# The norm's per-token scalars on VectorE: one-column operations with pointer scalars in place of four-column operations on two tensors

## The chip, the cores and the metric

The kernel runs on one core of one Trainium2 chip. The metric is the device time of one execution in microseconds (us). A core has TensorE (PE, matrix products into PSUM), VectorE (DVE), ScalarE (ACT), GpSimd (POOL), SyncE (SP, which here only issues DMAs) and DMA queues; each engine works through its own instructions in order and waits for semaphores of the others.

## What is computed

Three stages follow one another on 8 batches of 3072 tokens with 256 features: a filter in the frequency domain along the sequence, a feed-forward block whose activation is a softmax times its input followed by a layer norm without bias, and a feed-forward block that takes the maximum of three products.

```
X = np.fft.rfft(x, axis=1);  Y = X * F;  x = np.fft.irfft(Y)     # x: 8 x 3072 x 256
h = x @ w_in                                                      # 24576 x 1024
e = np.exp(h - max(h));  sm = e / (sum(e) + 1e-9)
solu = h * sm
ln = (solu - mean(solu)) / np.sqrt(var(solu) + 1e-6) * g_ln
x = ln @ w_out                                                    # 24576 x 256
h = max(x @ w1, x @ w2, x @ w3)                                   # 24576 x 768
out = h @ w_out2                                                  # 24576 x 256
```

The change touches the second stage: the small per-token numbers that stand in for the softmax's sum and the norm's variance.

## The kernel before, in words

**Tiling.** The sequence transform is done as products with small tables (items a, b, c, d). Six groups of 512 tokens make a batch, so there are 48 groups, numbered t = 0 to 47. For each group there are four h items of 128 tokens each (h0 to h3; `h_item`, L444), two z items (the product with the first w_out, L540), six m items (the three products with w1, w2, w3, L557) and two o items (the output, L587). Values are carried as two fp16 halves, so one logical product is three matmuls.

**What one h item does.** Twelve matmuls fill a PSUM tile `hps` (L461 to L463; one such buffer). VectorE takes its row maximum (L472) and scales it (L475); ScalarE forms the exponential and its row sum into `st[:, 0]` (L478). VectorE makes the scale of the product, `st[:, 1]` and `mx[:, 0]`, from the maximum with four one-column operations (L482 to L485) and multiplies: `u` (L489). Then the statistics of `u` (L493, L494), and the variance is copied into column i of `st[:, 2]` (L495). After h3 the four columns of the group are combined in three operations on 128 x 4 elements (L497 to L499), whose operands lie in SBUF: L497 reads `st[:, 0]` and `st[:, 1]`, L498 reads `st[:, 3]` twice, L499 reads `st[:, 4]` and `st[:, 2]`. GpSimd raises `st[:, 5]` to the power -0.5 (L500), multiplies by a constant (L585), and the o items use the result as a scale when ScalarE evicts them (L601).

**The other users of the same engines.** ScalarE makes the high half `uh` of `u` (L508) and GpSimd the low half `ul` (L509, two tensors of 128 x 1024 in SBUF). Of an m item, ScalarE evicts the first product into `am` (L574), VectorE takes the maximum with the other two (L576, twice), ScalarE makes the high half of `h` (L579) and GpSimd the low half (L580, two tensors in SBUF; for the last m item VectorE does it).

**The d item.** It fills two PSUM tiles `dps` (L424 to L426), which ScalarE (L432) and VectorE (L433, the low half of `y`) read. They come out of a ring of six PSUM tiles that the m, z, o and transform items share. So a later m item finds its PSUM tile free only when L433 has read the d item's tile: PE's matmuls of line L568 then wait for `y` L433.

**The order.** The order in which items are issued for a group is a string of the kernel, `z0 s0 z1 s1 h2 m0 x0 x0 x1 m1 x0 x0 m2 s2 x2 h3 m3 d m4 m5 g0 f o0 s3 o2 g1 s4`, in which s are steps of the next batch's transform, and g0, g1 are the items h0 and h1 of the group after next. In the code the statistics of an h item (`bn`, L491) are held until the next h item. The order on each engine is not that of the code: a scheduler places each operation by its priority and by when its inputs are expected, when the program is built. A change in a few operations can therefore move others.

Of the kernel before, what the change touches and what calls it, by code (L numbers as in the profile page):

```python
# [13 lines left out]
ALU = mybir.AluOpType  # L14
# [16 lines left out]
def kernel(  # L31
# [19 lines left out]
    V, S, G, PE, SP = nc.vector, nc.scalar, nc.gpsimd, nc.tensor, nc.sync  # L51
# [37 lines left out]
    def rtile(name):  # L89
        return ps_r.tile([128, 512], F32, tag="r", name=name)  # L90
# [353 lines left out]
    def h_item(b, g, i):  # L444
        y = y_t[b, g]
        sc = scl[b]
        if i == 0:
            st_t[b, g] = tiny.tile([128, 8, 4], F32, tag="st", name="st", bufs=3)
        st = st_t[b, g]
        if (b, g, i) in ((0, 0, 1), (0, 0, 3)):  # L450

            parts = [rtile("hps0"), rtile("hps1")]
        else:
            parts = [ps_h.tile([128, 1024], F32, tag="h", name="hps")]
        n = len(parts)
        tk = slice(i * 128, (i + 1) * 128)
        for f in range(2):
            o = parts[f % n][:, f * 512 * (2 - n):f * 512 * (2 - n) + 512]
            w = slice(f * 512, (f + 1) * 512)
            for dc in range(2):  # L460
                PE.matmul(o, y[:, dc, 0, tk], win[:, 0, dc, w], start=(dc == 0), stop=False)  # L461
                PE.matmul(o, y[:, dc, 0, tk], win[:, 1, dc, w], start=False, stop=False)  # L462
                PE.matmul(o, y[:, dc, 1, tk], win[:, 0, dc, w], start=False, stop=(dc == 1))  # L463
        u = two.tile([128, 1024], F32, tag="u", name="u")
        mx = tiny.tile([128, 4], F32, tag="mx", name="mx")
        mv = tiny.tile([128, 14], F32, tag="mv", name="mv")
        c1 = slice(i, i + 1)
        us = [u[:, k * 1024 // n:(k + 1) * 1024 // n] for k in range(n)]

        def early():  # L470
            for k, ps in enumerate(parts):
                V.tensor_reduce(mx[:, k:k + 1], ps, axis=AX.X, op=ALU.max)  # L472
            if n > 1:
                V.tensor_tensor(mx[:, 0:1], mx[:, 0:1], mx[:, 1:2], op=ALU.max)
            V.tensor_scalar(mx[:, 1:2], mx[:, 0:1], sc[:, 2:3], None, op0=ALU.mult)  # L475
            sums = [st[:, 0, c1], mx[:, 2:3]]
            for k, ps in enumerate(parts):
                S.activation(us[k], ps, AF.Exp, bias=mx[:, 1:2], scale=sc[:, 1:2], accum_out=sums[k])  # L478
            if bn_held[0]:
                bn_held[0]()  # L480
            bn_held[0] = bn
            V.tensor_scalar(st[:, 1, c1], mx[:, 0:1], sc[:, 1:2], 1.0, op0=ALU.mult, op1=ALU.max)  # L482
            V.tensor_tensor(st[:, 1, c1], st[:, 1, c1], mx[:, 1:2], op=ALU.max)
            V.reciprocal(st[:, 1, c1], st[:, 1, c1])
            V.tensor_scalar(mx[:, 0:1], st[:, 1, c1], sc[:, 3:4], None, op0=ALU.mult)  # L485
            if n > 1:
                V.tensor_tensor(sums[0], sums[0], sums[1], op=ALU.add)
            for k, ps in enumerate(parts):
                V.scalar_tensor_tensor(us[k], ps, mx[:, 0:1], us[k], op0=ALU.mult, op1=ALU.mult)  # L489

        def bn():  # L491
            for f in range(2):
                V.bn_stats(mv[:, 6 * f:6 * f + 6], u[:, f * 512:(f + 1) * 512])  # L493
            V.bn_aggr(mv[:, 12:14], mv[:, 0:12])  # L494
            V.tensor_copy(st[:, 2, c1], mv[:, 13:14])  # L495
            if i == 3:
                V.scalar_tensor_tensor(st[:, 3], st[:, 0], 1e-9, st[:, 1], op0=ALU.add, op1=ALU.mult)  # L497
                V.tensor_tensor(st[:, 4], st[:, 3], st[:, 3], op=ALU.mult)  # L498
                V.scalar_tensor_tensor(st[:, 5], st[:, 4], 1e-6 * 2.0 ** 26, st[:, 2], op0=ALU.mult, op1=ALU.add)  # L499
                G.tensor_tensor(st[:, 6], st[:, 5], mhalf, op=ALU.pow)  # L500

        def late():
            if i == 0:
                ln_t[b, g] = two.tile([128, 2, 8, 512], F16, tag="ln", name="ln")
            ln = ln_t[b, g]
            uh = two.tile([128, 1024], F16, tag="uh", name="uh")
            ul = two.tile([128, 1024], F16, tag="ul", name="ul")
            S.activation(uh, u, AF.Copy)  # L508
            (V if (b, g, i) == (0, 0, 3) else G).tensor_tensor(ul, u, uh, op=ALU.subtract)  # L509
            SP.dma_start_transpose(out=ln[:, 0, :, tk], in_=uh)  # L510
            SP.dma_start_transpose(out=ln[:, 1, :, tk], in_=ul)
        return early, late

    def z_parts(b, g):
# [520 lines left out]
    def h(i):  # L1035
        run(h_item(0, 0, i))
        flush()
# [67 lines left out]
    for t in range(NT):  # L1105
# [8 lines left out]
        def h(i):  # L1114
            if nxt:
                run(h_item(*nxt, i))
# [9 lines left out]
        for w in (ORDER if t else FIRST).split():  # L1126
            k, i = w[0], int(w[1:] or 0)
            if k == "h":
                h(i)
            elif k == "g" and nx2:  # L1130
                run(h_item(*nx2, i))
            elif k == "z":
                run(z_item(b, c, i))
                if i == 0:
                    fill(3)
            elif k == "m":
                m(i)
            elif k == "s":
                fft(i)
            elif k == "o":  # L1140
                run(o_item(b, c, i))
            elif k == "d" and nx2:
                run(d_item(*nx2))
            elif k == "f":
                flush()
            elif k == "x":
                if i == 0:
                    fill(1)
                    if not jobs and NB > 1 and 1 not in x_t and t == 0:
                        for k in range(6):  # L1150
                            load_x(1, k)
                if i == 1 and nx2 and nx2[1] == 0:
                    flush()
                    load_d(*nx2)
                if i == 2:
                    fin(b, c)
# [125 lines left out]
```

## Time and profile before

| | |
|---|---|
| time, median of 3 runs (lowest to highest) | 2904.94 us (2900.44 to 2908.57) |
| the profiled execution | 2904.83 us, of which its span from the first to the last instruction 2903.1 us |
| PE busy | 2804.4 us (97%) |
| DVE busy | 2048.4 us (71%) |
| ACT busy | 1236.9 us (43%) |
| POOL busy | 1139.9 us (39%) |
| granted TensorE clock, mean of the span | 0.992 of the upper level, 2.4 GHz |

PE is busy nearly all the time, so the views that matter are those that say where PE stands idle and who ends that idle time. A row of the waits names the engine, the operation that waited and what it waited for; a row of the timeline gives an operation's start, its duration, and in brackets the idle time of its engine ahead of it. In the timeline consecutive operations of one engine overlap a little, since they are pipelined.

### The profile page before, as it was taken

The numbers are of one execution on the slowest core, as the hardware profiler recorded it, in microseconds if no ns is written. First come the engines' busy times: TensorE is split into PE (matmuls) and PEld (weight loads), VectorE is DVE, ScalarE is ACT, GpSimd is POOL, SyncE is SP. The second block draws the span as 40 slices with busy tenths as digits, with TensorE's granted clock in tenths as the row PEclk, the third lists the DMA queues.
The fourth block names the chain that finished last, engine by engine and source line by source line (L and its number), as shares of the span: only waits on it lengthen the run. The fifth ranks groups of instructions, "written<-read, shape, count | busy, mean of one in ns | idle before, by whom it ended". The sixth has DMA issues, their size and how long they took to land.

```text
span 2903.1 us, 49134 instructions
## 1 busy us (share of the span) xinstructions
PE 2804.4 (97%) x18923; PEld 1561.0 (54%) x18924; DVE 2048.4 (71%) x3918; ACT 1236.9 (43%) x2024; POOL 1139.9 (39%) x1208
## 2 busy tenths in 40 slices
PE   8789899999999999999999999999999999999999
PEld 7544455555555555555555555555555555555555
DVE  7877668677777777777677767867777667656663
ACT  5644444344443344444444444434444344434332
POOL 5433553344334442344334433344432434323322
PEclk9999999999999999999999999999999999999999
DMA  8446885587467764677555875567844566422321
GB/s 256 107 102 166 146 177 156 102 138 130 104 157 125 134 116 106 162 126 130 113 146 121 134 125 118 153 110 134 136 110 107 112 137 117 92 66 52 62 48 29
DMA packets 718378, 352.71 MB, mean 121 GB/s; under 512 B 620544, under 2 KB 663936, under 8 KB 718144
## 3 DMA queue, kind: packets, MB, share of 16 engines
q1 hardware_dynamic: 689040, 242.57, 43.7%
q0 software_dynamic: 28960, 106.95, 15.0%
q8 instruction: 148, 2.42, 0.3%
q14 instruction: 86, 0.70, 0.1%
q10 hardware_dynamic: 144, 0.07, 0.0%
HBM read 126.13 MB, written 71.30 MB: 68 GB/s over the span
## 4 chain that ended last, share of the span: by engine, by line
PE 76%; DVE 11%; issue 4%; DMA 4%; POOL 3%; ACT 2%; SPq 0%; POOLq 0%; ACTq 0%; DVEq 0%
PE mps L568 10%; PE mps L570 9%; PE mps L569 9%; PE zps L548 5%; PE zps L551 5%; PE zps L549 5%; PE hps L461 5%; PE hps L462 5%; PE hps L463 5%; PE ops L596 4%; PE ops L597 4%; PE ops L595 4%; DVE st L497 2%; DVE am L576 2%; DVE mx L472 1%
## 5 line engine op out<-in xcount | busy, mean ns | idle before, releaser
L509 POOL TENSOR_TENSOR ul<-u,uh 128x1024 f16<-128x1024 f32 x191 | 408.2, 2137 | 1049.3 <-ACT uh L508 901.2
L568 PE MATMUL mps<-z,wm 128*128 128x512 f16 x1728 | 657.1, 380 | 45.2 <-DVE y L433 36.9
L569 PE MATMUL mps<-z,wm 128*128 128x512 f16 x1728 | 657.3, 380 | 0.0
L570 PE MATMUL mps<-z,wm 128*128 128x512 f16 x1728 | 657.1, 380 | 0.0
L576 DVE SCALAR_TENSOR_TENSOR am<-mps,am 128x512 f32<-128x512 f32 x576 | 393.7, 684 | 191.3 <-PE mps L570 96.3
L472 DVE TENSOR_REDUCE mx<-hps 128x1 f32<-128x1024 f32 (+1 forms) x194 | 234.5, 1209 | 213.3 <-PE hps L463 213.2
L579 ACT ACTIVATE h<-am 128x512 f16<-128x512 f32 x288 | 180.5, 627 | 464.1 <-DVE am L576 464.0
L580 POOL TENSOR_TENSOR h<-am,h 128x512 f16<-128x512 f32 x240 | 278.4, 1161 | 206.4 <-ACT h L579 205.8
L478 ACT ACTIVATE u<-hps,mx,scl 128x1024 f32<-128x1024 f32 (+1 forms) x194 | 231.7, 1195 | 290.5 <-DVE mx L475 242.1
L597 PE MATMUL ops<-wo,h 128*128 128x256 f16 x1152 | 314.1, 273 | 0.8 <-POOL h L580 0.8
L595 PE MATMUL ops<-wo,h 128*128 128x256 f16 x1152 | 314.0, 273 | 0.7 <-ACT o L601 0.6
L596 PE MATMUL ops<-wo,h 128*128 128x256 f16 x1152 | 314.1, 273 | 0.0
L461 PE MATMUL hps<-win,y 128*128 128x512 f16 x768 | 294.1, 383 | 13.3 <-ACT y L436 7.4
L569 PEld LDWEIGHTS <-wm 128*128 128x128 f16 x1728 | 169.4, 98 | 250.9 <-issue 58.2
L489 DVE SCALAR_TENSOR_TENSOR u<-hps,mx,u 128x1024 f32<-128x1024 f32 (+1 forms) x194 | 246.5, 1271 | 74.1 <-ACT u L478 72.9
L462 PE MATMUL hps<-win,y 128*128 128x512 f16 x768 | 294.0, 383 | 0.0
L463 PE MATMUL hps<-win,y 128*128 128x512 f16 x768 | 293.2, 382 | 0.0
L548 PE MATMUL zps<-ln,wo 128*128 128x512 f16 x752 | 285.8, 380 | 0.4 <-ACT o L601 0.4
L549 PE MATMUL zps<-ln,wo 128*128 128x512 f16 x752 | 285.7, 380 | 0.0
L508 ACT ACTIVATE uh<-u 128x1024 f16<-128x1024 f32 x192 | 202.8, 1056 | 192.8 <-DVE u L489 191.8
L570 PEld LDWEIGHTS <-wm 128*128 128x128 f16 x1728 | 169.5, 98 | 205.4 <-issue 2.7
L568 PEld LDWEIGHTS <-wm 128*128 128x128 f16 x1728 | 169.4, 98 | 199.8 <-issue 2.4
(233 smaller groups left out, 4500.3 us busy)
## 6 DMA issues: line engine op xcount, KB each, us to landing
out_dram<-o SPq DMA_DIRECT2D x95, 256.0 KB, 2.3
ft<-in_filt_dram POOLq DMA_DIRECT2D x56, 384.0 KB, 7.0
xt<-in_x_dram POOLq DMA_DIRECT2D x42, 512.0 KB, 8.4
scr_a<-ao SPq DMA_DIRECT2D x42, 512.0 KB, 3.3
bin<-scr_a POOLq DMA_DIRECT2D x56, 384.0 KB, 6.1
scr_z<-zt SPq DMA_DIRECT2D x56, 384.0 KB, 3.0
din<-scr_z POOLq DMA_DIRECT2D x42, 512.0 KB, 5.1
bt<-in_dft_b_dram POOLq DMA_DIRECT2D x56, 144.0 KB, 3.3
```

The source lines that it names most:

```text
L461: PE.matmul(o, y[:, dc, 0, tk], win[:, 0, dc, w], start=(dc == 0), stop=False)
L462: PE.matmul(o, y[:, dc, 0, tk], win[:, 1, dc, w], start=False, stop=False)
L463: PE.matmul(o, y[:, dc, 1, tk], win[:, 0, dc, w], start=False, stop=(dc == 1))
L548: PE.matmul(ps, wo1[:, 0, c, w], ln[:, 0, c], start=(c == 0), stop=False)
L549: PE.matmul(ps, wo1[:, 1, c, w], ln[:, 0, c], start=False, stop=False)
L568: PE.matmul(pss[k], wm[k][:, 0, dc, w], z[:, dc, 0], start=(dc == 0), stop=False)
L569: PE.matmul(pss[k], wm[k][:, 1, dc, w], z[:, dc, 0], start=False, stop=False)
L570: PE.matmul(pss[k], wm[k][:, 0, dc, w], z[:, dc, 1], start=False, stop=(dc == 1))
L576: V.scalar_tensor_tensor(am, ps, 2.0 ** -15, am, op0=ALU.mult, op1=ALU.max)
L595: PE.matmul(o, h2[:, j, 0, tk], wo2[:, 0, j], start=(j == 0), stop=False)
L596: PE.matmul(o, h2[:, j, 0, tk], wo2[:, 1, j], start=False, stop=False)
L597: PE.matmul(o, h2[:, j, 1, tk], wo2[:, 0, j], start=False, stop=(j == 5))
```

## The change

```
-            V.tensor_scalar(st[:, 1, c1], mx[:, 0:1], sc[:, 1:2], 1.0, op0=ALU.mult, op1=ALU.max)
-            V.tensor_tensor(st[:, 1, c1], st[:, 1, c1], mx[:, 1:2], op=ALU.max)
+            V.tensor_scalar(st[:, 1, c1], mx[:, 0:1], sc[:, 1:2], mx[:, 1:2], op0=ALU.mult, op1=ALU.max)
+            V.tensor_scalar(st[:, 1, c1], st[:, 1, c1], 1.0, None, op0=ALU.max)
             V.reciprocal(st[:, 1, c1], st[:, 1, c1])
...
             for k, ps in enumerate(parts):
                 V.scalar_tensor_tensor(us[k], ps, mx[:, 0:1], us[k], op0=ALU.mult, op1=ALU.mult)
+            V.tensor_scalar(st[:, 3, c1], st[:, 0, c1], 1e-9, st[:, 1, c1], op0=ALU.add, op1=ALU.mult)
+            V.tensor_scalar(st[:, 4, c1], st[:, 3, c1], st[:, 3, c1], 1e-6 * 2.0 ** 26, op0=ALU.mult, op1=ALU.mult)
 
         def bn():
...
             V.bn_aggr(mv[:, 12:14], mv[:, 0:12])
-            V.tensor_copy(st[:, 2, c1], mv[:, 13:14])
+            V.tensor_scalar(st[:, 5, c1], mv[:, 13:14], st[:, 4, c1], None, op0=ALU.add)
             if i == 3:
-                V.scalar_tensor_tensor(st[:, 3], st[:, 0], 1e-9, st[:, 1], op0=ALU.add, op1=ALU.mult)
-                V.tensor_tensor(st[:, 4], st[:, 3], st[:, 3], op=ALU.mult)
-                V.scalar_tensor_tensor(st[:, 5], st[:, 4], 1e-6 * 2.0 ** 26, st[:, 2], op0=ALU.mult, op1=ALU.add)
                 G.tensor_tensor(st[:, 6], st[:, 5], mhalf, op=ALU.pow)
```

The three four-column operations of a group become three one-column operations of each h item: the second input is given as a pointer scalar (one value for each partition), so each reads one tensor. The same is done to L483: the maximum with `mx[:, 1]` moves into L482 as its second pointer scalar. The new lines are L490, L491 (behind `u`) and L497 (behind the aggregate, in place of the copy); line numbers from L495 on shift: statistics are L495 and L496 in the new kernel, the maximum of an m item is L575, the low half of its last item L579.

The order on VectorE ahead of `y` L433, in a group of the steady part, before (st: the small numbers, mv: statistics, am: an m item's maximum):

```order
L576 SCALAR_TENSOR_TENSOR am<-mps,am 128x512
L493 BN_STATS mv<-u 128x6 x2
L497 SCALAR_TENSOR_TENSOR st<-st 128x4
L494 BN_AGGR mv<-mv 128x2
L498 TENSOR_TENSOR st<-st 128x4
L495 COPY st<-mv 128x1
L433 TENSOR_TENSOR y<-dps,y 128x512 x2
L499 SCALAR_TENSOR_TENSOR st<-st 128x4
```

and the same place in the changed kernel, behind `u` L489:

```order
L490 TENSOR_SCALAR st<-st 128x1
L575 SCALAR_TENSOR_TENSOR am<-mps,am 128x512
L491 TENSOR_SCALAR st<-st 128x1
L495 BN_STATS mv<-u 128x6 x2
L433 TENSOR_TENSOR y<-dps,y 128x512 x2
L496 BN_AGGR mv<-mv 128x2
L497 TENSOR_SCALAR st<-mv,st 128x1
```

Ahead of `y` the two operations on four columns, the aggregate and the copy are gone, and two one-column operations have come.

The order on VectorE in the first group (t = 0) around `u` of h3, before (xm: maxima of the next batch's input, which wait for its load):

```order
L484 RECIPROCAL st<-st 128x1
L111 TENSOR_REDUCE xm<-xt 128x1
L485 TENSOR_SCALAR mx<-st,scl 128x1
L497 SCALAR_TENSOR_TENSOR st<-st 128x4
L111 TENSOR_REDUCE xm<-xt 128x1
L489 SCALAR_TENSOR_TENSOR u<-hps,mx,u 128x1024
```

and the same place in the changed kernel, from `u` on:

```order
L489 SCALAR_TENSOR_TENSOR u<-hps,mx,u 128x1024
L490 TENSOR_SCALAR st<-st 128x1
L575 SCALAR_TENSOR_TENSOR am<-mps,am 128x512
L491 TENSOR_SCALAR st<-st 128x1
L495 BN_STATS mv<-u 128x6 x2
L111 TENSOR_REDUCE xm<-xt 128x1
```

The reductions of the next batch's input stood ahead of `u` and now stand behind it. On PE the order of items is the same from group 1 on; in the first group and ahead of it some matmuls trade places with their neighbours.

## Rows read from the trace of the kernel before

**Rows 1.** The page: span, and busy time, share, instructions of each engine.

```profile
span 2903.1 us, 49134 instructions
PE 2804.4 (97%) x18923; PEld 1561.0 (54%) x18924; DVE 2048.4 (71%) x3918; ACT 1236.9 (43%) x2024; POOL 1139.9 (39%) x1208
```

**Rows 2.** Waits of PE, whole span: us in total, times, longest us.

```profile
PE mps L568 <- DVE y L433: 36.9, 26, 2.9
PE hps L461 <- ACT y L436: 7.4, 1, 7.4
PE bps L242 <- DMA bin<-scr_a: 6.8, 1, 6.8
PE hps L461 <- DVE u L489: 6.0, 3, 4.2
```

**Rows 3.** Timeline of PE at three of these waits: start, duration, [idle before].

```profile
560.87 0.38 PE L568 MATMUL mps<-z,wm 128*128 128x512 f16 x1 [1.54 <-DVE y L433]
...
1023.18 0.38 PE L570 MATMUL mps<-z,wm 128*128 128x512 f16 x1
1025.08 0.38 PE L568 MATMUL mps<-z,wm 128*128 128x512 f16 x1 [1.52 <-DVE y L433]
...
2356.40 0.58 PE L568 MATMUL mps<-z,wm 128*128 128x512 f16 x1 [2.93 <-DVE y L433]
```

**Rows 4.** Timeline of DVE ahead of the first of them.

```profile
1017.08 0.21 DVE L475 TENSOR_SCALAR mx<-mx,scl 128x1 f32<-128x1 f32 x1
1017.21 0.20 DVE L482 TENSOR_SCALAR st<-mx,scl 128x1 f32<-128x1 f32 x1
1017.44 0.16 DVE L483 TENSOR_TENSOR st<-st,mx 128x1 f32<-128x1 f32 x1
...
1020.45 1.28 DVE L493 BATCH_NORM_STATS2 mv<-u 128x6 f32<-128x512 f32 x2
1021.64 1.61 DVE L497 SCALAR_TENSOR_TENSOR st<-st 128x4 f32<-128x4 f32 x1
1023.18 0.20 DVE L494 BATCH_NORM_AGGREGATE mv<-mv 128x2 f32<-128x12 f32 x1
1023.30 1.07 DVE L498 TENSOR_TENSOR st<-st 128x4 f32<-128x4 f32 x1
1024.29 0.14 DVE L495 COPY st<-mv 128x1 f32<-128x1 f32 x1
1024.36 1.27 DVE L433 TENSOR_TENSOR y<-dps,y 128x512 f16<-128x512 f32 x2
```

**Rows 5.** Timeline of POOL at the same time.

```profile
1021.12 2.12 POOL L509 TENSOR_TENSOR ul<-u,uh 128x1024 f16<-128x1024 f32 x1 [4.73 <-ACT uh L508]
1023.20 1.15 POOL L580 TENSOR_TENSOR h<-am,h 128x512 f16<-128x512 f32 x1
```

**Rows 6.** Timeline of ACT: the high half of y, there and in another group.

```profile
1021.45 1.06 ACT L432 ACTIVATE y<-dps 128x512 f16<-128x512 f32 x2
...
500.17 1.06 ACT L432 ACTIVATE y<-dps 128x512 f16<-128x512 f32 x2
```

**Rows 7.** Timeline of DVE in that other group, where POOL did not compute.

```profile
500.36 0.15 DVE L497 SCALAR_TENSOR_TENSOR st<-st 128x4 f32<-128x4 f32 x1
500.61 0.11 DVE L498 TENSOR_TENSOR st<-st 128x4 f32<-128x4 f32 x1
500.79 1.28 DVE L433 TENSOR_TENSOR y<-dps,y 128x512 f16<-128x512 f32 x2
```

**Rows 8.** The small operations: count, ns min/median/max, first and last start, forms.

```profile
L482 DVE TENSOR_SCALAR st<-mx,scl x192: 160/204/207, 96.5 to 2839.7; 128x1 f32<-128x1 f32 x192
L485 DVE TENSOR_SCALAR mx<-st,scl x192: 198/214/216, 98.0 to 2840.3; 128x1 f32<-128x1 f32 x192
L495 DVE COPY st<-mv x192: 140/153/156, 101.2 to 2847.3; 128x1 f32<-128x1 f32 x192
L497 DVE SCALAR_TENSOR_TENSOR st<-st x48: 145/1616/3453, 126.2 to 2844.6; 128x4 f32<-128x4 f32 x48
L498 DVE TENSOR_TENSOR st<-st x48: 107/1068/1076, 126.4 to 2846.3; 128x4 f32<-128x4 f32 x48
```

**Rows 9.** The first group: timeline of PE, then of DVE.

```profile
179.72 0.61 PE L461 MATMUL hps<-win,y 128*128 128x512 f16 x1 [4.20 <-DVE u L489]
```

```profile
175.71 1.22 DVE L111 TENSOR_REDUCE xm<-xt 128x1 f32<-128x1024 f32 x1 [1.20 <-DMA xt<-in_x_dram]
178.38 1.27 DVE L489 SCALAR_TENSOR_TENSOR u<-hps,mx,u 128x1024 f32<-128x1024 f32 x1
```

## Prediction

> **What bounds the kernel now.** The first view is the table of busy times: PE works 2804.4 of 2903.1 us, VectorE 2048.4 [rows 1]. VectorE as a whole is not the bound, so what the change takes from or gives to its busy time counts for nothing by itself; only operations that stand ahead of something PE waits for count. PE is idle for 2903.1 - 2804.4 = 98.7 us, and that is the most that any change off PE can win. The second view, the waits of PE, says who ends that idle time: 36.9 us in 26 waits for `y` L433, and otherwise single waits of the start and of the first batch, 7.4, 6.8 and 6.0 us [rows 2]. The third view is the timeline around one of the 26. PE ran out of work behind a matmul begun at 1023.18 and went on at 1025.08, idle for 1.52 us; the longest such wait is 2.93 us, and of the others none is over 1.54 us [rows 3]. What VectorE did meanwhile: the statistics at 1020.45, then L497, which took 1.61 us for four elements per partition, the aggregate, L498 with 1.07 us, the copy, and at 1024.36 `y` [rows 4]. PE waits for work of which two tiny operations are the largest part.
>
> Why do they take so long? GpSimd's `ul` runs from 1021.12 to 1023.24, and L497 ends at 1021.64 + 1.61 = 1023.25; GpSimd's L580 runs from 1023.20 to 1024.35, and L498 ends at 1023.30 + 1.07 = 1024.37 [rows 4, 5]. Both operations end with a GpSimd operation on two SBUF tensors. In a group where GpSimd did not compute at that moment, L497 took 0.15 us and L498 0.11 us [rows 7]. So an operation of VectorE with two SBUF tensors is held until GpSimd's is through. The one-tensor operations show nothing of it: in 192 cases each, L482 never took more than 0.207 us, L485 0.216 us, the copy L495 0.156 us, where L497 has a median of 1.616 us [rows 8].
>
> **The change part by part.** *What leaves the path to `y`.* From the end of the statistics (L497 starts at 1021.64) to `y` (1024.36) VectorE spent 2.72 us [rows 4]. In the new order all four operations of that stretch are gone from it: L497 and L498 don't exist any more, the aggregate and what follows it stand behind `y`.
>
> *What is added to it.* L490 and L491 stand ahead of `y`. Each has one tensor and one pointer scalar, like L482, and takes a place of 0.13 us (from L475 at 1017.08 to L482 at 1017.21) [rows 4]: 0.26 us for both. L482 now reads `mx[:, 1]`, which L475 has written just before; a step that depends on the one ahead takes 0.23 us (L482 at 1017.21, L483 at 1017.44) instead of 0.13 [rows 4], so 0.10 us more. Its second pointer scalar has no row of its own: from below it is free, and from above I take the whole duration of such an operation again, 0.2 us [rows 8]; I take nothing, since L482 with one pointer and a constant is no longer than L485 with one pointer alone. L483 with a constant in place of a tensor stays at one place. So VectorE is ready for `y` at 1021.64 + 0.26 + 0.10 = 1022.00.
>
> *What is late next.* `y` needs ScalarE's high half. ScalarE begins that at 1021.45 [rows 6]; where VectorE was early, `y` began 500.79 - 500.17 = 0.62 us behind it [rows 6, 7]. ScalarE itself follows `u`, which L482 makes 0.10 us later. So `y` begins at 1021.45 + 0.10 + 0.62 = 1022.17, not 1024.36: 2.19 us sooner. 25 of the 26 waits are at most 1.54 us and go entirely, with 0.65 us to spare; of the one of 2.93 us 0.74 us is left. Gain: 36.9 - 0.74 = 36.2 us. The spare 0.65 us also covers the 0.2 us that a second pointer might cost. In the groups without a wait nothing is won.
>
> *The other h items.* Each gets 0.13 us twice behind `u` and 0.10 us ahead of it. PE waits for `u` only 6.0 us in 3 waits, all in the first group and ahead of it [rows 2], so in the steady part the time before the next h item hides them. If that cover were gone, 0.36 us x 192 = 69 us would be at stake, but the row of PE's waits names no such wait. The last combination is now one column behind the aggregate instead of L499, off PE's path.
>
> *The first group.* The scheduler also moves other work there. Before, `u` of h3 stood behind reductions of the next batch's input that waited for a load (1.20 us at 175.71), `u` came at 178.38, and PE stood 4.20 us until 179.72 [rows 9]. In the new order the reductions stand behind `u`. The most that this wins is 4.2 us; but PE then comes sooner to the next batch's first item, which waited 6.8 us for its load already [rows 2], so the time may be given back. From below I allow a loss of one more wait of that kind, 6.8 us. I take half of the gain, 2.1 us.
>
> *The sum.* The profiled execution took 2904.83 us, 1.7 us more than its span and within 0.2 us of the median 2904.94, so it stands for it. 2904.8 - 36.2 - 2.1 = 2866.5 us.
>
> **One rule against the change.** The rows show no one-tensor operation held by GpSimd [rows 8]. The Trainium skill, page "SBUF — State Buffer", section "Who interferes with whom", agrees on operations with two SBUF inputs, but says that copies and `tensor_scalar` too can enter a mode that uses both ports and then contend with GpSimd. By that rule the new operations would be held as well, and the sum would be rival C's; by the rows it is the forecast. 192 copies and 384 `tensor_scalar` of one column speak against it here.
>
> **The rivals.** *B, half of it.* ScalarE becomes the bound of `y`: its high half of `y` is already the last to be ready, 0.17 us behind VectorE, and its queue is in order. If PE, now without pauses, finds it about 1.4 us later than in the old phase, then 0.75 us of a typical wait of 1.42 (36.9 / 26) comes back: 26 x 0.75 = 19 us, and the time is about 2886. Against it: ScalarE is busy 43% [rows 1] and is fed by PE, so it moves along with it.
>
> *C, the stall stays.* The one-column operations are held by GpSimd like the old ones, and L490 and L491 pay ahead of `y` what L497 and L498 paid (1.54 and 0.99 us as places in the timeline). Then `y` begins 2.72 - 2.53 - 0.10 = 0.09 us sooner, the gain is 26 x 0.09 = 2.3 us, and the time 2904.8 - 2.3 - 2.1 = 2900.4, no measurable change. The change would then not do what it says. For it: nothing but the rule above. Against it: [rows 8], and that GpSimd begins `ul` only at 1021.12, behind the place of the new pair.
>
> *D, slower.* A pointer scalar that an operation just ahead has written could cost more than a tensor read: VectorE might have to fetch it only when the write has landed. The place is L482, L490 and L491 of each h item; no row shows such a pair alone. Ahead of `y` three such reads stand, so with a price p each the 2.19 us are used up at p = 0.73 us, and at p = 1.0 us `y` is 0.81 us later than before: 26 x 0.81 = 21 us, 2904.8 + 21 - 2 = 2924. It decides from p = 0.85 on, at which the loss leaves the noise. Against it: L485, which reads what the reciprocal has just written, as a tensor, takes 0.214 us in all [rows 8].
>
> *E, more.* The first group keeps all of its 4.2 us and some of its other waits shrink: 2860 or less.
>
> **How the numbers follow.** About 0.3% (8.7 us) is what a measurement of this kernel can tell from no change. The forecast, 2861 to 2873, has 73%; E, below it, 6%; B, 2874 to 2896, 12%; C 5%; D 4%. Faster by over 0.3% (below 2896) is the forecast with B and E, 91%; within it C, 5%; slower D, 4%. The range 2857 to 2879 holds the forecast's cases, nearly all of E and the nearer part of B, some 80%; its lower end is 36.9 + 4.2 us plus the 6.8 us of the first batch's load, its upper end the forecast with a loss of 6.8 us in the start and a few tenths of a us left at each wait.
>
> **What would show it.** In the profile after: PE's waits for `y` fall from 36.9 us to a few us; the timeline shows statistics, then `y`, some 2.2 us sooner against PE; no small operation on `st` over 0.3 us beside GpSimd's `ul`; L490 and L491 at about 0.2 us each in 192 cases. The sum is wrong if the 26 waits stay with another name (B: ScalarE's L432), if the new operations have durations that end with GpSimd's (C) or are long without GpSimd (D), or if the start moves by more than 7 us.

## The result, and the profile after

The changed kernel takes 2859.46 us (median of 4 runs, 2854.47 to 2866.93) against 2906.76 us before (2900.44 to 2908.96); the ratio is 0.9843, with a 95% interval of 0.9816 to 0.9870. Predicted were 2866.5 us, from 2857 to 2879; the likeliest band of the prediction, 2861 to 2873, begins 1.5 us above the median. The profiled execution of the changed kernel is the slowest of its four: 2866.93 us, a span of 2865.1 us, 38.0 us less than the span of [rows 1].

The busy times of the changed kernel, in the form of [rows 1] (engine, us, share of the span, instructions):

```profile
span 2865.1 us, 49331 instructions
PE 2801.6 (98%) x18923; PEld 1567.6 (55%) x18924; DVE 2000.6 (70%) x4158; ACT 1237.0 (43%) x2024; POOL 1138.6 (40%) x1208
```

VectorE has 240 more instructions and is 48 us less busy. PE does the same work. What matters is its waits, in the form of [rows 2] (us in total, times, longest us), of the whole span:

```profile
PE cps L377 <- ACT am L573: 8.4, 1, 8.4
PE hps L461 <- ACT y L436: 6.5, 1, 6.5
PE bps L242 <- DMA bin<-scr_a: 6.5, 1, 6.5
...
PE mps L567 <- DVE y L433: 0.6, 1, 0.6
```

The 26 waits for `y` of [rows 2], 36.9 us, have become one of 0.6 us. All others here lie in the first 480 us. The group of [rows 4] in the changed kernel, on VectorE, then on GpSimd and ScalarE (start, duration):

```profile
1011.06 0.21 DVE L475 TENSOR_SCALAR mx<-mx,scl 128x1 f32<-128x1 f32 x1
1011.30 0.27 DVE L482 TENSOR_SCALAR st<-mx,scl 128x1 f32<-128x1 f32 x1
1011.61 0.15 DVE L483 TENSOR_SCALAR st<-st 128x1 f32<-128x1 f32 x1
...
1014.64 0.20 DVE L491 TENSOR_SCALAR st<-st 128x1 f32<-128x1 f32 x1
1014.76 1.28 DVE L495 BATCH_NORM_STATS2 mv<-u 128x6 f32<-128x512 f32 x2
1016.13 1.29 DVE L433 TENSOR_TENSOR y<-dps,y 128x512 f16<-128x512 f32 x2
1017.34 0.20 DVE L496 BATCH_NORM_AGGREGATE mv<-mv 128x2 f32<-128x12 f32 x1
1017.57 0.21 DVE L497 TENSOR_SCALAR st<-mv,st 128x1 f32<-128x1 f32 x1
```

```profile
1015.18 2.12 POOL L508 TENSOR_TENSOR ul<-u,uh 128x1024 f16<-128x1024 f32 x1 [4.82 <-ACT uh L507]
1017.27 1.15 POOL L579 TENSOR_TENSOR h<-am,h 128x512 f16<-128x512 f32 x1
```

```profile
1015.52 1.06 ACT L432 ACTIVATE y<-dps 128x512 f16<-128x512 f32 x2
```

`y` starts 1.37 us behind the start of the statistics instead of 3.91 [rows 4]. GpSimd's `ul` still runs across that stretch, but nothing on VectorE is held by it: L497 runs while GpSimd's L579 does, and takes 0.21 us.

**Where the time went.** From the first m matmul of group 5 to that of group 47 the kernel before needs 2389.62 us (478.37 to 2867.99 in PE's timeline), the changed one 2346.84 (483.24 to 2830.08): 42.8 us less. PE's busy time in these stretches, before and after, in the table of stretches (stretch, length, busy us of PE, PEld, DVE, ACT, POOL with instructions, granted clock, DMA share, GB/s; mean of the one stretch not shown):

```profile
478.00:2868.00 2390.00, 2352.90 (x15812) 1283.23 (x15811) 1692.64 (x3221) 991.26 (x1619) 915.14 (x938) 1.00 0.59 116
```

```profile
483.00:2830.00 2347.00, 2346.36 (x15810) 1282.77 (x15809) 1648.05 (x3427) 990.78 (x1619) 914.78 (x938) 1.00 0.58 118
```

In the changed kernel PE is busy 2346.4 of 2347 us. There is nothing left to win in this part without taking work from PE. From the first m matmul of group 47 to the end it is 35.1 us in both. The spans differ by less than the steady part because 4.9 us are lost ahead of group 5: 483.2 us against 478.4.

### The profile page after: what moved, and what is told of

Same layout as the page of the kernel before. It is cut to its first block, busy times and chain, and to the rows that moved or that the text cites. A ratio compares the mean times of both kernels' runs of the same rounds, so it can differ in the third digit from the quotient of the medians.

```text
span 2865.1 us, 49331 instructions
## 1 busy us (share of the span) xinstructions
PE 2801.6 (98%) x18923; PEld 1567.6 (55%) x18924; DVE 2000.6 (70%) x4158; ACT 1237.0 (43%) x2024; POOL 1138.6 (40%) x1208
## 4 chain that ended last, share of the span: by engine, by line
PE 90%; DMA 3%; POOL 2%; DVE 2%; issue 2%; ACT 1%; SPq 0%; ACTq 0%; POOLq 0%; DVEq 0%
PE mps L567 12%; PE mps L569 12%; PE mps L568 12%; PE hps L461 6%; PE hps L462 6%; PE hps L463 5%; PE zps L547 5%; PE zps L550 5%; PE zps L548 5%; PE ops L596 4%; PE ops L595 4%; PE ops L594 4%; DMA ft<-in_filt_dram 1%; PE bps L242 1%; PE bps L243 1%
## 5 line engine op out<-in xcount | busy, mean ns | idle before, releaser
L575 DVE SCALAR_TENSOR_TENSOR am<-mps,am 128x512 f32<-128x512 f32 x576 | 395.1, 686 | 211.2 <-PE mps L569 129.0
L579 POOL TENSOR_TENSOR h<-am,h 128x512 f16<-128x512 f32 x240 | 278.1, 1159 | 188.5 <-ACT h L578 185.7
L489 DVE SCALAR_TENSOR_TENSOR u<-hps,mx,u 128x1024 f32<-128x1024 f32 (+1 forms) x194 | 246.4, 1271 | 51.5 <-ACT u L478 48.8
```

## Experiments

The theory: L497 and L498 were held because GpSimd worked on two SBUF tensors at that moment; they stood ahead of `y`, for which PE waits; the change takes held operations out of that place. The first rivals: the gain comes from the two-tensor maximum L483 in all 192 h items; two-tensor operations are slow wherever they stand; the start is worth a part of it. "Steady part" is the stretch from group 5 to group 47 above. In each profile its length is read from PE's timeline, and it turned out to repeat within 0.2 us for one and the same kernel, where whole times scatter by 10 us.

**again.** The changed kernel unchanged.

> The changed kernel once more, to separate its steady part from its start. My theory (two operations with two SBUF tensors ahead of y are held until GpSimd's operation on two SBUF tensors ends; without them PE's waits for y go) expects PE's waits for y at 0.6 us as in the first profile, the steady part the same to 1 us, and a time of 2854 to 2867, the spread of its four runs so far, with any difference of the span made before 250 us. If the profiled start (clock 0.88 in the first 100 us against 0.95 before) was chance, the start differs here; if it is the new order, it is the same.

Measured: 2868.39 us (2867.12 to 2870.01), ratio 0.9868 (0.9845 to 0.9890). Steady part 2346.85 us, group 5 reached at 484.5 us. The steady part is exactly that of the first profile. The median is 9 us higher than in the first series; the two profiled executions, 2866.93 and 2868.16 us, differ only ahead of group 5. The other executions have no trace, so that theirs differ there too is likely but not shown.

**only_max.** The first part of the change alone.

```
-            V.tensor_scalar(st[:, 1, c1], mx[:, 0:1], sc[:, 1:2], 1.0, op0=ALU.mult, op1=ALU.max)
-            V.tensor_tensor(st[:, 1, c1], st[:, 1, c1], mx[:, 1:2], op=ALU.max)
+            V.tensor_scalar(st[:, 1, c1], mx[:, 0:1], sc[:, 1:2], mx[:, 1:2], op0=ALU.mult, op1=ALU.max)
+            V.tensor_scalar(st[:, 1, c1], st[:, 1, c1], 1.0, None, op0=ALU.max)
```

> Only the first part of the change: the maximum with mx moves into L482 as a second pointer scalar, L483 takes a constant; the three four-column operations stay. The order on VectorE is that of before. My theory: L497 and L498 are held as before (medians 1.6 and 1.07 us), PE waits for y 37 to 42 us (L482 a little longer), time 2902 to 2910. Rival, the gain comes from the two-tensor maximum in all 192 items: some 20 us or more of it are seen here, 2885 or less.

Measured: 2906.77 us, ratio 1.0004 (0.9989 to 1.0019). PE's waits in the steady part:

```profile
PE mps L568 <- DVE y L433: 40.3, 27, 3.0
```

That is 3.4 us more than before, and the steady part takes 2392.63 us, 3.0 us more. This part of the change brings nothing and costs 3 us: L482 with two pointer scalars takes 0.273 us in place of 0.204, and most of the waits are 0.08 us longer. Against what I expected, the order on VectorE is not quite that of before. The operations ahead of `y` are the same, but in groups 11, 17 and 23, where others trade places, the wait has grown by 0.2 to 0.6 us.

**only_st.** The second part alone: L490, L491 and L497 as in the change, L482 and L483 as before.

> Only the second part: the three four-column operations become one-column ones with pointer scalars; L482 and L483 stay as before (L483 with two tensors). My theory: all of the gain, PE waits for y under 1 us, time 2854 to 2867, L482 back at 0.204 us. Rival (the maximum is what counts): 2885 or more.

Measured: 2864.15 us, ratio 0.9849 (0.9825 to 0.9873); steady part 2346.76 us, waits for `y` 0.8 us in 2. All of the gain in the steady part is here, and the rival of the maximum falls.

**two_tensors.** The new operations at their new places, one column each, but with two SBUF tensors.

```
-            V.tensor_scalar(st[:, 3, c1], st[:, 0, c1], 1e-9, st[:, 1, c1], op0=ALU.add, op1=ALU.mult)
-            V.tensor_scalar(st[:, 4, c1], st[:, 3, c1], st[:, 3, c1], 1e-6 * 2.0 ** 26, op0=ALU.mult, op1=ALU.mult)
+            V.scalar_tensor_tensor(st[:, 3, c1], st[:, 0, c1], 1e-9, st[:, 1, c1], op0=ALU.add, op1=ALU.mult)
+            V.tensor_tensor(st[:, 4, c1], st[:, 3, c1], st[:, 3, c1], op=ALU.mult)
...
-            V.tensor_scalar(st[:, 5, c1], mv[:, 13:14], st[:, 4, c1], None, op0=ALU.add)
+            V.scalar_tensor_tensor(st[:, 5, c1], st[:, 4, c1], 1e-6 * 2.0 ** 26, mv[:, 13:14], op0=ALU.mult, op1=ALU.add)
```

> The changed kernel with the new operations per h item, one column each, but each reading two SBUF tensors instead of one tensor and a pointer scalar. The pair behind u stands ahead of y as in the changed kernel. My theory: being held depends on what GpSimd runs at that moment; behind u, and ahead of ul, which needs u first, GpSimd seldom computes, so the pair ahead of y takes about 0.15 us in most h3 items and y comes as early as in the changed kernel but for the aggregate (0.12 us): waits for y 1 to 8 us, time 2857 to 2872; the last one, behind y, is held by ul and has durations over 1 us. Rival, two tensors are slow wherever they stand: the pair costs what L497 and L498 did, waits for y over 30 us, time 2895 or more.

Measured: 2872.74 us, ratio 0.9882 (0.9858 to 0.9906); steady part 2347.96 us, waits for `y` 1.1 us in 2. The three operations (count, ns min/median/max, first and last start):

```profile
L490 DVE SCALAR_TENSOR_TENSOR st<-st x192: 143/149/779, 101.2 to 2807.3; 128x1 f32<-128x1 f32 x192
L491 DVE TENSOR_TENSOR st<-st x192: 141/147/493, 102.5 to 2808.0; 128x1 f32<-128x1 f32 x192
L497 DVE SCALAR_TENSOR_TENSOR st<-st,mv x192: 143/1460/3683, 104.8 to 2810.2; 128x1 f32<-128x1 f32 x192
```

All three have two tensors and one column. The pair behind `u`, where GpSimd has mostly not begun `ul`, has medians of 0.15 us; the third, behind the aggregate, is held to a median of 1.46 us. It stands behind `y`, and the whole steady part is only 1.1 us longer than in the changed kernel. So being held depends on the moment, and its cost on the place. The second rival falls. Nearly all of the gain comes without pointer scalars: it was enough that the pair stands behind `u`, one column each. Four columns in that place were not tried.

**dummy_two and dummy_one.** The changed kernel with one operation more in each group, right ahead of `y`, whose result nobody uses: with two SBUF tensors, or with one.

```
             if i == 3:
+                V.scalar_tensor_tensor(st[:, 2], st[:, 0], 1e-9, st[:, 1], op0=ALU.add, op1=ALU.mult)      # dummy_two
+                V.tensor_scalar(st[:, 2], st[:, 0], 1e-9, 1.0, op0=ALU.add, op1=ALU.mult)                  # dummy_one
                 G.tensor_tensor(st[:, 6], st[:, 5], mhalf, op=ALU.pow)
```

> The changed kernel with one more operation for each group, whose result nobody uses: four columns, two SBUF tensors, right ahead of y on VectorE. Everything else stands in the same order. My theory: it is held until ul of GpSimd ends. In the trace of the changed kernel VectorE is free for y at 1015.96 and ul ends at 1017.30, so it takes about 1.3 us, y comes 1.1 us later (1.1 of the 2.2 us won), 17 waits of about 0.4 us, 5 short ones and one of 1.8 come back: 8 to 11 us of waits for y, steady part 2357 to 2360 us (2346.8 without it), time 8 to 14 us over the changed kernel. Rival (L497 and L498 were slow by themselves, or the gain comes from the aggregate's place): 0.15 us, steady part within 1 us of 2346.8.

> The same with one SBUF tensor and two constants in place of two tensors, at the same place, four columns. My theory: not held, 0.15 us, waits for y 0.6 to 1.5 us, steady part within 1 us of 2346.8. Rival (any four-column operation there is held, or one-tensor operations too contend with GpSimd): as with two tensors.

Measured: dummy_two 2877.07 us, ratio 0.9913 (0.9886 to 0.9939), steady part 2360.89 us; dummy_one 2882.17 us, ratio 0.9923 (0.9897 to 0.9949), steady part 2360.68 us. PE's waits in the steady part, and the place in the timeline, first dummy_two:

```profile
PE mps L568 <- DVE y L433: 10.6, 20, 1.7
...
1018.31 1.37 DVE L499 SCALAR_TENSOR_TENSOR st<-st 128x4 f32<-128x4 f32 x1
...
1017.54 2.12 POOL L509 TENSOR_TENSOR ul<-u,uh 128x1024 f16<-128x1024 f32 x1 [4.81 <-ACT uh L508]
```

then dummy_one:

```profile
PE mps L568 <- DVE y L433: 10.2, 19, 1.7
...
1017.88 1.38 DVE L499 TENSOR_SCALAR st<-st 128x4 f32<-128x4 f32 x1
...
1017.11 2.12 POOL L509 TENSOR_TENSOR ul<-u,uh 128x1024 f16<-128x1024 f32 x1 [4.82 <-ACT uh L508]
```

dummy_two is as the theory expects: held until `ul` ends (1017.54 + 2.12 = 1019.66; 1018.31 + 1.37 = 1019.68), 14 us back, a steady part 0.9 us over the top of what I gave. dummy_one is not: an operation with one tensor and two constants is held as long (to 1019.26, with `ul` ending at 1019.23). So "one tensor" is not what keeps the new operations free. A new theory: it is the one column. The rows at hand agree. L490 and L491 say little, since in the changed kernel only 2 and 7 of their 192 cases start while GpSimd has more than 0.15 us of `ul` or of a low half of `h` left to do; but L497 starts so in 172 of 192 cases and never takes more than 0.216 us:

```profile
L497 DVE TENSOR_SCALAR st<-mv,st x192: 197/214/216, 105.9 to 2807.9; 128x1 f32<-128x1 f32 x192
```

The next experiment tests it at the same spot.

**dummy_column.** As dummy_one, on one column.

```
-                V.tensor_scalar(st[:, 2], st[:, 0], 1e-9, 1.0, op0=ALU.add, op1=ALU.mult)
+                V.tensor_scalar(st[:, 2, c1], st[:, 0, c1], 1e-9, 1.0, op0=ALU.add, op1=ALU.mult)
```

> As dummy_one (an extra tensor_scalar with one tensor and two constants right ahead of y, which took 1.38 us with four columns), now on one column. My theory after that run: a tensor_scalar is held when it has four columns and not when it has one: 0.07 to 0.2 us, waits for y 0.6 to 1.5 us, steady part within 1 us of 2346.8. Rival (the place alone decides, whatever stands there is held): 1.3 us and 2360.

Measured: a single execution of 2857.84 us, so no interval; steady part 2346.85 us. The operation in dummy_one, then in dummy_column (48 cases each), and the wait in dummy_column:

```profile
L499 DVE TENSOR_SCALAR st<-st x48: 118/1382/3791, 127.4 to 2818.3; 128x4 f32<-128x4 f32 x48
```

```profile
L499 DVE TENSOR_SCALAR st<-st x48: 100/134/142, 127.8 to 2797.8; 128x1 f32<-128x1 f32 x48
...
PE mps L568 <- DVE y L433: 0.6, 1, 0.6
```

With one column the same operation at the same place never takes more than 0.142 us, though in 41 of the 48 cases `ul` is running when it starts, as in dummy_one. Four columns cost 14 us over the kernel, one column nothing.

**before_again, old_start, after_5, old_start_5.** The start. before_again is the kernel before. old_start uses the old form in batch 0 and the new form from batch 1 on (each changed line under `if b:`, the old one under `else:`); its order on PE, ScalarE and GpSimd is that of before, and on VectorE up to batch 1.

> The kernel before once more, for a second profile of its start. The time is that of before. From the first m item of group 5 on, the steady part takes 2389.6 us as in its first profile, to 1 us. If the order in the start is what costs the changed kernel some 5 us there, group 5 is again reached at about 474 to 479 us (first profile of before 478.4, the kernel with only the maximum changed 473.8; the changed kernel 483.2 and 484.5). If those differences are chance, 483 or more is as likely.

> The changed form for batches 1 to 7 and the old form for batch 0. The order on PE, ScalarE and GpSimd is then that of before throughout, on VectorE until batch 1. My theory (steady part gains 42.8 us, the new order in the start loses about 5): group 5 reached at 474 to 479 us, steady part 2347 us as in the changed kernel, time 2857 to 2863, some 5 us under the changed kernel and 43 to 46 under before. Rival (the start differs by chance): as the changed kernel, about 2868 on the chip of the last runs.

> The changed kernel beside the one with the old start, on one chip with five rounds. Steady part 2346.8 us; group 5 reached at 480 to 485 us; time 2857 to 2869. If the new order in the start costs some 5 us, it is slower than the one with the old start by 3 to 7 us; if the start is chance (granted clock in the first 140 us), the two agree within 2 us.

> Old form in batch 0, new form in batches 1 to 7, as before (old_start), with five rounds. Steady part 2346.8 us. If the new order in the start costs some 5 us: 2855 to 2863 and 3 to 7 us under the changed kernel of this call; if chance: the same as that within 2 us.

| | time, us (lowest to highest) | ratio to before | group 5 reached, us | steady part, us |
|---|---|---|---|---|
| before, first profile | 2904.94 | | 478.4 | 2389.62 |
| before_again | 2902.16 (2897.64 to 2913.91) | 1.0000 (0.9983 to 1.0017) | 473.9 | 2389.78 |
| only_max | 2906.77 (2901.22 to 2911.83) | 1.0004 (0.9989 to 1.0019) | 473.8 | 2392.63 |
| after, first profile | 2859.46 (2854.47 to 2866.93) | 0.9843 (0.9816 to 0.9870) | 483.2 | 2346.84 |
| again | 2868.39 (2867.12 to 2870.01) | 0.9868 (0.9845 to 0.9890) | 484.5 | 2346.85 |
| after_5 | 2859.01 (2857.09 to 2861.32) | 0.9838 (0.9815 to 0.9862) | 477.6 | 2346.85 |
| old_start | 2861.11 (2856.84 to 2866.12) | 0.9853 (0.9826 to 0.9880) | 482.4 | 2346.85 |
| old_start_5 | 2861.79 (2852.36 to 2868.70) | 0.9845 (0.9820 to 0.9871) | 468.6 | 2346.84 |

My expectation of 5 us for the order in the start was not confirmed: the same kernel, old_start, reached group 5 at 482.4 us in one execution and at 468.6 in another, and beside each other after_5 and old_start_5 have medians of 2859.0 and 2861.8 us with overlapping runs. One thing that goes along with it is the granted clock of the first 140 us; the two profiles of that one kernel (old_start, then old_start_5) have

```profile
0.00:140.00 140.00, 111.10 (x841) 96.94 (x843) 101.63 (x215) 78.34 (x134) 62.64 (x92) 0.87 0.61 179
```

```profile
0.00:140.00 140.00, 111.44 (x889) 91.86 (x890) 109.00 (x227) 87.17 (x150) 68.54 (x96) 0.95 0.63 186
```

a clock of 0.87 with 841 matmuls done, and 0.95 with 889. Ahead of group 5 PE is busy for 429.1 and 416.6 us with the same matmuls, which is 12.5 of the 13.7 us between the two. PE's idle time there, the stretch less the busy time, goes more by the order: 57.5 to 61.7 us in five of six profiles with the order of the changed kernel (after, again, after_5, the dummies; dummy_column has 52.7), and 52.1 to 53.5 in four of five with that of before (before, before_again, old_start, old_start_5, on_gpsimd; the first profile of before has 57.8). So a loss of some 5 us in the new order is not excluded, but the times of whole runs do not show it, and it stays open.

**on_gpsimd.** The kernel before, with the combination of the group on GpSimd.

```
-                V.scalar_tensor_tensor(st[:, 3], st[:, 0], 1e-9, st[:, 1], op0=ALU.add, op1=ALU.mult)
-                V.tensor_tensor(st[:, 4], st[:, 3], st[:, 3], op=ALU.mult)
-                V.scalar_tensor_tensor(st[:, 5], st[:, 4], 1e-6 * 2.0 ** 26, st[:, 2], op0=ALU.mult, op1=ALU.add)
+                G.tensor_scalar(st[:, 3], st[:, 0], 1e-9, None, op0=ALU.add)
+                G.tensor_tensor(st[:, 3], st[:, 3], st[:, 1], op=ALU.mult)
+                G.tensor_tensor(st[:, 4], st[:, 3], st[:, 3], op=ALU.mult)
+                G.tensor_scalar(st[:, 4], st[:, 4], 1e-6 * 2.0 ** 26, None, op0=ALU.mult)
+                G.tensor_tensor(st[:, 5], st[:, 4], st[:, 2], op=ALU.add)
```

> The kernel before with the combination of the group given to GpSimd (five operations on four columns, behind the variance of h3) and nothing else changed; VectorE keeps the copy, L482 and L483 are old. No pointer scalars. My theory (what counts is that no operation held by GpSimd stands ahead of y): aggregate and copy stand ahead of y (0.2 us in place of the 0.26 us of L490 and L491), waits for y about 0.6 us, steady part 2346 to 2348 us, time 2855 to 2869. GpSimd's five operations take 0.3 to 1.1 us each, beside PE. Rival (GpSimd then comes late with the low halves of h, which the o items need): waits of PE for L580's rows, steady part 2355 or more.

Measured: 2866.18 us (2856.34 to 2869.75), ratio 0.9856 (0.9831 to 0.9882); steady part 2346.50 us, one wait for `y` of 0.7 us. GpSimd's operations are shorter than I expected, 0.2 us each:

```profile
L498 POOL TENSOR_TENSOR st<-st x48: 198/199/217, 120.0 to 2793.3; 128x4 f32<-128x4 f32 x48
```

A third form with the same steady part: it is enough that no operation which GpSimd holds stands ahead of `y`. The aggregate and the copy still stand ahead of `y` here, so the gain does not come from their new place. None of these kernels is faster than the changed one by more than the scatter of the start.

## Why the prediction was right, and where it was not

**The bound and the cause: right.** The waits for `y` were the steady part's only idle time in the list of waits, and the two four-column operations ahead of it were the cause. dummy_two brings 14 of the 43 us back by putting one such operation in that place again; only_st has all of the gain without the maximum.

**The path to `y`: right, to 0.02 us.** I had `y` 2.19 us sooner against PE's work. Measured from the first m matmul of group 14 (997.94 before, 991.92 after, in PE's timeline), `y` came 26.42 us later before and 24.21 after: 2.21 us sooner. ScalarE's high half is what `y` now waits for, 0.61 us ahead of it, as the prediction said. Of the 2.93 us wait 0.74 us were to be left; 0.64 are.

**The price of the waits: too small by 6.5 us.** This term was mis-sized. I took the bracketed idle time, 36.9 us, as what the waits cost. Of it 36.3 us went, and the steady part became 42.8 us shorter. The other 6.5 us stand in the rows of the stretches above as PE's busy time, 2352.90 us before and 2346.36 after for the same matmuls, and the lengths of the groups show where they come from:

- *The overlap, 3.6 us.* Idle time runs from the modelled end of the last matmul, 0.38 us after its start, while in an unbroken row matmuls start 0.216 us apart. A break shown as 1.52 us [rows 3] moves the next start from 0.22 to 1.90 us behind the last one and so costs 1.68: 0.16 us more than shown. In five groups it is 0.09 us.
- *The clock, 1.4 us.* It fell behind the longest break (below).
- *Breaks that are not listed, 1.5 us.* In eleven more groups (10, 16, 22, 23, 28, 34, 35 and 40 to 43) the matmul that waits for `y` began 0.31 to 0.53 us behind the last one, with too little idle time for the list. These groups became 0.09 to 0.31 us shorter. One of them before:

```profile
2581.64 0.38 PE L570 MATMUL mps<-z,wm 128*128 128x512 f16 x1
2582.04 0.38 PE L568 MATMUL mps<-z,wm 128*128 128x512 f16 x1
```

**The start: no gain shown.** I had taken 2.1 us of a possible 4.2. The wait for `u` at 179.72 [rows 9] is gone in the changed kernel, and a new one stands in its place, on PE and the operation that VectorE was at:

```profile
188.71 0.28 PE L596 MATMUL ops<-wo,h 128*128 128x256 f16 x1 [3.98 <-DVE h L579]
```

```profile
186.83 1.22 DVE L111 TENSOR_REDUCE xm<-xt 128x1 f32<-128x1024 f32 x1 [3.09 <-DMA xt<-in_x_dram]
```

The reductions that wait for the next batch's load now stand ahead of the low half of `h` and not of `u`; PE waits 3.98 us for that, and 4.77 and 4.75 us in the profiles of again and after_5. The wait was handed on, not removed. Of the 4.9 us lost ahead of group 5, 3.5 are busy time of PE for the same matmuls, at a clock of 0.88 in the first 140 us where the profile of before had 0.95.

**Luck in the sum.** In the profiled execution the errors of the two terms nearly cancel, so that 2866.93 us stands beside a forecast of 2866.5: in the steady part 42.8 us gained where I had 36.2, ahead of it 4.9 us lost where I had 2.1 gained. That is luck. The other three executions are 6.9 to 12.5 us shorter, and the median came out 7 us below the forecast. Since the steady part repeats to 0.2 us in the traces, this is most likely the start, but those executions have no trace. The median, 2859.46 us, lies below the band that had 73% and in that of rival E (2860 or less, 6%), and not for E's reason: no gain of the start is shown, and what was larger is the price of the waits.

**The pointer scalars: the second one is not free.** L482 takes 0.273 us instead of 0.204, and the next step starts 0.31 us behind it (1011.30 to 1011.61) in place of 0.23. I had taken nothing and allowed 0.2. It cost nothing here, since ScalarE is the later one for `y`; in only_max it is about 2 of the 3 us.

```profile
L482 DVE TENSOR_SCALAR st<-mx,scl x192: 249/273/276, 101.7 to 2801.9; 128x1 f32<-128x1 f32 x192
L490 DVE TENSOR_SCALAR st<-st x192: 197/205/214, 102.9 to 2804.9; 128x1 f32<-128x1 f32 x192
L491 DVE TENSOR_SCALAR st<-st x192: 196/203/209, 104.2 to 2805.6; 128x1 f32<-128x1 f32 x192
```

L490 and L491 took the 0.2 us that were expected. They do not test rival D, since on VectorE another operation always stands between them. L482 does: in 152 of 192 cases it stands directly behind L475, which writes its second pointer, and takes 0.272 to 0.276 us; in the other 40 it takes 0.249 to 0.269. So a pointer just written costs at most some 0.03 us where D needs 0.85: rival D falls.

**The rivals.** B (ScalarE takes over): it is the later one now, but it begins the high half of `y` only 0.09 us later against PE (23.60 us behind the first m matmul of group 14 instead of 23.51), not 1.4.

C: not here, but mostly not for the reason that I gave first. Of the rows that I set against it, L482 and L485 prove nothing: in the kernel before not one of their 192 cases each starts while GpSimd computes `ul` or a low half of `h`. The copy L495 starts with more than 0.15 us of them left in 131 of 192 cases and was a fair test, for one column. What kept the pair ahead of `y` free is the second argument, that it stands ahead of `ul`: in two_tensors it had two tensors each and took 0.15 us there. And "one tensor" is not enough: dummy_one shows that with four columns such an operation is held for 1.38 us. The Trainium skill, page "SBUF — State Buffer", section "Who interferes with whom", counts `tensor_scalar` among the operations that can contend with GpSimd, when its operands meet certain conditions, and dummy_one agrees with it. The prediction left these conditions out when it said that by the rule the new operations would be held as well. By that rule a rewrite to one tensor on four columns in that place would have been no remedy, and that is what the 1.38 us show.

## What to carry to other kernels

A tiny operation with a duration ten times its smallest is probably waiting; lay the other engines' timelines beside it and look what ends when it ends. Then ask where it stands: only the ones ahead of something that the bounding engine waits for count, and moving them ahead of the contending operation can help as much as rewriting them (here to within 1.1 us). Where an engine is the bound, compare start to start across a break, since the idle time shown leaves out the overlap that the break destroys; and compare stretches of the steady part, which here repeat to 0.2 us where whole times scatter by 10.

## What the runs showed of the hardware

**Being held by GpSimd goes by form and width.** While GpSimd's two-tensor operations ran, VectorE operations on `st` with two SBUF tensors were held at four columns (L497 and L498 [rows 8]; 1.37 us in dummy_two) and at one column (median 1.46 us in two_tensors); `tensor_scalar` with one tensor was held at four columns (1.38 us) and not at one (0.134 us, at most 0.142). Every case that was held for over 1 us (L497 and L498 before, the dummies) ends within 0.04 us of the end of a GpSimd operation on two tensors. The statistics, one tensor of 512 columns, were not held: 115 of the 384 start with more than 0.15 us of `ul` or of a low half of `h` left, and none takes more than 0.695 us:

```profile
L495 DVE BATCH_NORM_STATS2 mv<-u x384: 673/683/695, 104.4 to 2806.3; 128x6 f32<-128x512 f32 x192
```

Why one column escapes is not shown by these runs; two and three columns were not tried.

**The clock behind the longest break.** In the kernel before, after the wait of 2.93 us [rows 3], the granted clock of the next 3.6 us is 0.58 of the upper level, and for some seven matmuls the starts are 0.43 us apart instead of 0.216, the pace of the lower level, 1.2 GHz:

```profile
2356.40:2360.00 3.60, 3.60 (x10) 1.32 (x10) 2.31 (x5) 1.11 (x2) 2.19 (x3) 0.58 0.49 109
...
2358.06 0.63 PE L569 MATMUL mps<-z,wm 128*128 128x512 f16 x1
2358.48 0.63 PE L570 MATMUL mps<-z,wm 128*128 128x512 f16 x1
```

The breaks of 1.5 us show no such fall. In the changed kernel the break at that place is 0.64 us, the clock stays at 1.00, and this group is 3.68 us shorter, where the break itself explains 2.29.
